# Attention and routed experts on one core: low halves of P at seven other blocks, a reordered preparation, magnitude sums as bfloat16 products

## The chip, the core and the metric

The kernel runs on one core of a Trainium2 chip. The metric is device time in microseconds (us), the median over runs of one launch. TensorE is called PE, VectorE DVE, ScalarE ACT, GpSimd POOL and SyncE SP, as in the profile.

## What is computed

Attention over 8 batches of 8 heads, 1152 keys and 576 pooled queries of 64 columns, and then a layer of 8 experts over the 4608 rows that come out of it, each row sent to one expert.

```python
q_pool = q.reshape(B, H, S // 2, 2, D).mean(axis=3)
scores = (1 / sqrt(D)) * q_pool @ k^T
attn = exp(scores - max); attn /= attn.sum() + 1e-9
x = (attn @ v) as 4608 rows of 512
e = argmax(x @ w_gate); weight = softmax(x @ w_gate)[e]
out = weight * sigmoid(x @ w_output_gate)[e] * (relu(x @ w1[e]) @ w2[e])
```

## The kernel before, in words

The attention works on 32 *pairs* (a batch and two of its heads), counted from 0 here. A pair has 18 *blocks* (two heads, nine chunks of 128 keys), and the main loop (lines 706 to 736) makes one *step* for each block. PE, DVE, ACT and POOL execute exactly in the order in which this loop writes their instructions (line 686), so the place of a call in a step is its place in the queue of its engine.

In a step, `scores` (lines 429 to 455) makes the scores of a block transposed (keys by queries) in one of two PSUM buffers, `sps0` for even blocks and `sps1` for odd ones: two products of high halves (L440) and two of low halves and maxima (L442). ACT takes the exponential P (L444). Its bfloat16 high half is read in place; the low half `pl` is P minus the high half. At most blocks POOL makes it from SBUF (L452), and then the PSUM buffer is free again once ACT has read it. At the blocks of the table `PLP` ACT takes the exponential a second time into PSUM (L446), and DVE subtracts (L449), at the start of the next step; the PSUM buffer is then free only after DVE. The block two later waits for it.

Beside this a step has: one or two maximum tiles (`mgen`, lines 355 to 388: scores of the pair after, 128 queries by 384 keys, two or three matmuls on L377 and a maximum by DVE on L378), which go through three small PSUM banks in rotation; zero to three groups of 15 products with V (`av`, L467 to L469), six steps behind the scores; and `rows` (line 407), which transposes a finished set of maxima (L412) through one of the three banks and hands it on to a split on DVE in the next step. In odd steps there are two maximum tiles, in even ones one. `norm` (L476 to L478) divides a finished head; `logits` and `router` (lines 512 to 647) are run by it, the router once in four pairs, in the pair after a batch's last, which makes the order repeat every four pairs.

`prep` (lines 143 to 347) prepares a pair ahead of its use, and a table gives the third of a step at which each of its parts is written out: `PREPF`, `PREP0` and `PREP` for pair 0, pair 1 and the rest. Its parts that matter here: `lk` loads q and k; `kabs` (L209) sums the magnitudes of k on ACT; `gk` (L213) adds that sum over partitions by an fp32 product with `blk`, in a bank that is held until `ksc(1)` (L220); `ks`, `kh`, `qs`, `qh` scale and round on ACT, `kl`, `qsum`, `ql` on POOL; `dk`, `dq`, `dl` send the results to their places through SP. For V, `amax` (ACT), `gmax` (an fp32 product with `onesf`, L319), `scale`, `vh` (ACT), `vs` and `vl` (POOL) do the same. The parts for k of pair n run during pair n-2, those for V during pair n-1.

After the attention the expert layer runs tile by tile; its code is not touched.

Of the kernel before, what the change touches and what calls it, by code (L numbers as in the profile page):

```python
# [23 lines left out]
PREP0 = ((0, 'lk'), (6, 'qsum'), (8, 'kabs'), (11, 'gk'), (12, 'ksc', 0), (12, 'ksc', 1), (13, 'ksc', 2), (14, 'ks', 0), (15, 'kh', 0), (15, 'qs'), (16, 'ks', 1), (17, 'kh', 1), (18, 'qh'), (18, 'kl'), (19, 'ql'), (19, 'dq', 0), (20, 'dq', 1), (22, 'qd'), (23, 'sk', 0, 0), (26, 'sk', 0, 1), (29, 'sk', 1, 0), (32, 'sk', 1, 1), (28, 'dl', 0), (29, 'dl', 1),  # L24
# [48 lines left out]
def attention(tc, qT, kT, vL, wg, keep, xrows, idscr, cum, pairs, setup, scat, init, exps):  # L73
    nc = tc.nc
    nb = len(pairs) // 4
    with ExitStack() as ctx:
# [66 lines left out]
        def prep(n, table):  # L143
# [531 lines left out]
        def prep_at(s, ph):  # L675
            u = 3 * (s + SLEAD) + ph
            for n in range(max(u // 54 - 2, 0), min(u // 54 + 2, NP)):
                r = u - 54 * n + min(3 * (LEAD - 15), 2 * n)
                if r == 0:
                    preps[n] = prep(n, PREP if n > 1 else PREP0 if n else PREPF)  # L680
                if n in preps:
                    for f in preps[n].pop(r, ()):
                        f()

        E = mybir.EngineType
        with tc.manual_schedule(engines={E.PE, E.DVE, E.Activation, E.Pool}):
# [55 lines left out]
def keep_tiles(tc, kp, NT, NP_):  # L742
    nc = tc.nc
# [512 lines left out]
```

## Time and profile before

| what | value |
|---|---|
| median of 3 runs | 1489.22 us (1487.53 to 1489.45) |
| profiled execution | 1491.79 us |
| its span, first to last instruction | 1489.9 us |
| mean granted PE clock | 0.991 of 2.4 GHz |
| busy share of PE, DVE, ACT, POOL | 96%, 75%, 68%, 63% |

The span of the profiled execution is 1.9 us shorter than its time. The attention's X at 968 us; the experts fill the rest. The pairs of the steady part follow each other every 28.6 to 30.2 us, with the pattern of four named above (pairs 12 to 15, for example, begin at 386.24, 415.61, 445.77 and 474.80 us). Matmuls overlap each other in the pipeline of PE, so what one costs the stream is read from the start of one to the start of the next, not from its duration.

### The profile page before, as it was taken

How to read it: one execution, taken by the hardware profiler on the slowest of the kernel's cores; microseconds unless marked ns; L12 is line 12 of the kernel's file. 1: busy time of each engine (PE TensorE's matmuls, PEld its weight loads, DVE VectorE, ACT ScalarE, POOL GpSimd, SP SyncE). 2: the span in 40 equal slices, each digit the busy share in tenths (PEclk: the TensorE clock that was granted, in tenths of full speed). 3: DMA queues.
4: the chain of work that ended last, by engine and by line, in shares of the span. 5: the costliest groups of instructions: out<-in, count | busy, mean ns of one | idle time of the engine just before them, and what ended most of it. 6: DMA issues, size and time to landing. Idle time of an engine off the chain costs nothing. (4 is left out here: it accounts for less than half of the span.)

```text
span 1489.9 us, 40217 instructions
## 1 busy us (share of the span) xinstructions
PE 1431.0 (96%) x16044; PEld 1144.2 (77%) x16044; DVE 1117.9 (75%) x2438; ACT 1012.9 (68%) x1723; POOL 939.1 (63%) x892
## 2 busy tenths in 40 slices
PE   7899999999999999999999999889999999999996
PEld 4677777777777777777777777777888888888874
DVE  8678787887887787788787787576778778777752
ACT  5777778777877877777877776644655556556542
POOL 3877888788889779878879888663333233333200
PEclk9999999999999999999999999999999999999998
DMA  5445344444443453444244433148636665453550
GB/s 190 123 122 145 102 134 123 115 118 118 117 137 102 115 143 98 117 134 121 86 137 125 126 92 96 58 148 330 231 105 232 228 233 213 171 186 122 218 186 8
DMA packets 92047, 212.57 MB, mean 143 GB/s; under 512 B 13356, under 2 KB 28924, under 8 KB 91854
## 3 DMA queue, kind: packets, MB, share of 16 engines
q1 hardware_dynamic: 81262, 188.35, 40.8%
q0 software_dynamic: 9152, 20.85, 4.1%
q8 instruction: 128, 2.10, 0.6%
q10 hardware_dynamic: 1440, 0.74, 0.2%
q14 instruction: 65, 0.53, 0.1%
HBM read 164.23 MB, written 23.02 MB: 126 GB/s over the span
## 5 line engine op out<-in xcount | busy, mean ns | idle before, releaser
L378 DVE TENSOR_REDUCE pm<-mp 128x1 f32<-128x384 f32 x864 | 449.5, 549 | 114.2 <-PE mp L377 109.6
L444 ACT ACTIVATE p<-sps 128x576 f32<-128x576 f32 x576 | 375.8, 653 | 199.6 <-PE sps L442 180.7
L452 POOL TENSOR_TENSOR pl<-p 128x576 f16<-128x576 f32 x383 | 437.8, 1146 | 112.5 <-ACT p L444 94.0
L377 PE MATMUL mp<-ka,qa 128*128 128x384 f16 x960 | 297.3, 326 | 12.0 <-DVE pm L378 6.5
L467 PE MATMUL av<-vt,p 128*128 128x65 f16 x2880 | 291.8, 193 | 0.2 <-DVE xb L478 0.2
L468 PE MATMUL av<-vt,p 128*128 128x64 f16 x2880 | 291.5, 194 | 0.0
L469 PE MATMUL av<-vt,pl 128*128 128x65 f16 x2880 | 291.1, 192 | 0.0
L467 PEld LDWEIGHTS <-p 128*128 128x128 bf16 x2880 | 265.8, 97 | 20.8 <-DVE xb L478 4.4
L468 PEld LDWEIGHTS <-p 128*128 128x128 bf16 x2880 | 264.4, 97 | 14.0
L469 PEld LDWEIGHTS <-pl 128*128 128x128 f16 x2880 | 264.3, 98 | 0.0
L377 PE MATMUL mp<-kb,qb 66*128 66x384 f16 x768 | 250.7, 326 | 0.8 <-DVE kb L251 0.5
L440 PE MATMUL sps<-qa,ka 128*128 128x288 f16 x1152 | 235.9, 286 | 11.2 <-DVE pl L449 9.8
L958 PE MATMUL hps<-x,w1h 128*128 128x512 f32 (+1 forms) x704 | 230.7, 389 | 7.6 <-DVE x L942 3.4
L442 PE MATMUL sps<-qb,kb 69*128 69x288 f16 x1152 | 235.7, 285 | 0.0
L449 DVE TENSOR_TENSOR pl<-sps,p 128x576 f16<-128x576 f32 x193 | 146.2, 757 | 38.1 <-ACT sps L446 29.8
L958 PE MATMUL hps<-x,w1l 128*128 128x256 f32 (+1 forms) x704 | 165.4, 276 | 0.0
L960 ACT COPY hs<-hps 128x512 f32<-128x512 f32 (+1 forms) x88 | 49.0, 557 | 171.0 <-PE hps L958 171.0
L958 PEld LDWEIGHTS hps<-x,w1l 128*128 128x128 f32 x704 | 132.3, 190 | 13.0
L958 PEld LDWEIGHTS hps<-x,w1h 128*128 128x128 f32 x704 | 122.8, 190 | 23.9 <-DVE x L942 4.0
L442 PEld LDWEIGHTS <-kb 69*128 69x128 f16 x1152 | 112.7, 98 | 29.2
L377 PEld LDWEIGHTS <-qa 128*128 128x128 f16 x960 | 95.2, 99 | 46.8 <-issue 9.5
L790 POOL DMA_INDIRECT ids<-idscr,riD x36 | 44.8, 1244 | 134.4 <-DMA out_dram<-y,ids 123.1
(243 smaller groups left out, 2810.5 us busy)
## 6 DMA issues: line engine op xcount, KB each, us to landing
raw2b<-in_w_dram SPq DMA_DIRECT2D x24, 1024.0 KB
raw1b<-in_w_dram SPq DMA_DIRECT2D x24, 1024.0 KB
raw1a<-in_w_dram SPq DMA_DIRECT2D x22, 1024.0 KB
raw2a<-in_w_dram SPq DMA_DIRECT2D x22, 1024.0 KB
vp<-in_vL_dram SPq DMA_DIRECT2D x32, 576.0 KB
qp<-in_qT_dram SPq DMA_DIRECT2D x31, 576.0 KB
kpf<-in_kT_dram SPq DMA_DIRECT2D x31, 576.0 KB
ka<-xk SPq DMA_DIRECT2D x120, 144.0 KB
```

The source lines that it names most:

```text
L377: nc.tensor.matmul(mp, lhsT=l, rhs=r, start=j == 0, stop=j == len(ops) - 1)
L378: nc.vector.tensor_reduce(out=pm[:, i:i + 1], in_=mp, axis=AX.X, op=ALU.max)
L440: nc.tensor.matmul(sps[:, j, 0:288], lhsT=ka[:, h, ks], rhs=qa[:, o + 288 * j:o + 288 * j + 288], start=True, stop=False)
L442: nc.tensor.matmul(sps[:, j, 0:288], lhsT=kb[:, h, ks], rhs=qb[:, h, 288 * j:288 * j + 288], start=False, stop=True)
L444: e_ = nc.scalar.activation(out=p32.rearrange("p (j n) -> p j n", j=2), in_=x, func=AF.Exp, scale=1.0 / 16)
L449: nc.vector.tensor_tensor(out=pl.rearrange("p (j n) -> p j n", j=2), in0=x, in1=ph.rearrange("p (j n) -> p j n", j=2), op=ALU.subtract)
L452: nc.gpsimd.tensor_tensor(out=pl, in0=p32, in1=ph, op=ALU.subtract)
L467: nc.tensor.matmul(av_[:, qb, 0:65], lhsT=hi, rhs=vt[:, h, c, 0:65], start=c == 0 and qb == 0, stop=False)
L468: nc.tensor.matmul(av_[:, qb, 0:64], lhsT=hi, rhs=vt[:, h, c, 66:130], start=False, stop=False)
L469: nc.tensor.matmul(av_[:, qb, 0:65], lhsT=lo, rhs=vt[:, h, c, 0:65], start=False, stop=c == NC - 1 and qb == 4)
L958: nc.tensor.matmul(hp[:, f, 0:n], lhsT=W1[l][g][:, c, fs], rhs=d['x'][:, c, 0:n], start=c == 0 and l == 0, stop=c == 3 and l == 0)
L960: nc.scalar.copy(out=hs, in_=hp[:, :, w:2 * w])
```

## The change

Five parts:

- `PLP`, the blocks whose low half DVE makes, becomes (1, 3, 5, 7, 9, 12, 13) in place of (1, 3, 7, 9, 11, 13): block 5 comes in, and block 12 takes the place of block 11. It holds for pairs 0 to 30; pair 31 has a table of its own, unchanged.
- From pair 4 on, `prep` runs by a new table: `kabs` at 8 in place of 14 (six thirds, two steps, earlier), `ksc(1)` directly behind `ksc(0)`, `qh` two thirds later, and the parts `scale`, `vh`, `vs`, `vl` of V shifted by one or two thirds. Pairs 2 and 3 keep the old table under the name `PREPE`.
- `dl` is cut in two, `dkl` (low half of k) and `dql` (low half of q), and k's goes first.
- `gk` and `gmax` multiply the upper 16 bits of the sums, read as bfloat16, by a `blk` and a `ones` of bfloat16.
- From step 54 (pair 3) on, `rows` is called right after the routers and ahead of the scores of its step, where it stood behind the maximum tiles.

```diff
-PREPK = (... (12, 'qsum'), (14, 'kabs'), (20, 'gk'), (21, 'ksc', 0), (22, 'ksc', 1), ... (31, 'qh'), ... (38, 'dl', 0), (40, 'dl', 1))
-PREPV = ((63, 'lv'), (82, 'amax', 0), (88, 'amax', 1), (93, 'gmax'), (94, 'scale', 0), (95, 'scale', 1), (99, 'scale', 2), (100, 'vh', 0), (101, 'vs', 0), (103, 'vl', 0), (107, 'vh', 1), (107, 'vs', 1), (110, 'vl', 1))
-PREP = PREPK + tuple((r + FWD, *x) for r, *x in PREPV)
+PREP = (... (8, 'kabs'), (12, 'qsum'), (20, 'gk'), (21, 'ksc', 0), (21, 'ksc', 1), ... (33, 'qh'), ... (38, 'dkl', 0), (38, 'dql', 0), (40, 'dkl', 1), (40, 'dql', 1)) + tuple((r + FWD, *x) for r, *x in ((63, 'lv'), (82, 'amax', 0), (88, 'amax', 1), (93, 'gmax'), (95, 'scale', 0), (96, 'scale', 1), (100, 'scale', 2), (101, 'vh', 0), (102, 'vs', 0), (104, 'vl', 0), (105, 'vh', 1), (108, 'vs', 1), (111, 'vl', 1)))
-PLP = (1, 3, 7, 9, 11, 13)
+PLP = (1, 3, 5, 7, 9, 12, 13)
-                nc.tensor.matmul(g[:, 0:1], lhsT=blk, rhs=ak[:, 0:1], start=True, stop=True)
+                nc.tensor.matmul(g[:, 0:1], lhsT=blk, rhs=ak.bitcast(BF16)[:, 1:2], start=True, stop=True)
-            def dl(h):
-                r = slice(64 * h, 64 * h + 64)
+            def dkl(h):
+                dmaf(kb[0:64, h], kp[64 * h:64 * h + 64])
+
+            def dql(h):
                 o = h * (NQ + 64)
-                dmaf(qa[64:128, o:o + NQ], yq[r])
-                dmaf(kb[0:64, h], kp[r])
+                dmaf(qa[64:128, o:o + NQ], yq[64 * h:64 * h + 64])
-                nc.tensor.matmul(g, lhsT=onesf, rhs=am, start=True, stop=True)
+                nc.tensor.matmul(g, lhsT=ones, rhs=am.bitcast(BF16).rearrange('p (h t) -> p h t', t=2)[:, :, 1], start=True, stop=True)
-                    preps[n] = prep(n, PREP if n > 1 else PREP0 if n else PREPF)
+                    preps[n] = prep(n, PREP if n > 3 else PREPE if n > 1 else PREP0 if n else PREPF)
+                if s >= 54 and (s % 2 == 0):
+                    rows()
                 pop()
                 if live:
                     next(sg)
...
-                if s < 54 or s % 2 == 0:
+                if s < 54:
                     rows()
-    blk = t('blk', [128, 128], F32)
+    blk = t('blk', [128, 128], BF16)
```

How the rows move, at the three places that matter. First ACT in blocks 0 to 3 of pair 15; `p` is written by the first exponential of a block, `vt` by `vh`, `kjunk` by `kabs`. Before:

```order
L444 ACTIVATE p_10542<-sps_10544 128x576
L332 ACTIVATE vt_147<-vp,sc 128x9x64
L444 ACTIVATE p_10588<-sps_10590 128x576
L446 ACTIVATE sps_10590<-sps_10590 128x2x288
L444 ACTIVATE p_10607<-sps_10609 128x576
L209 ACTIVATE kjunk,ak<-kpf 128x1152
L444 ACTIVATE p_10658<-sps_10660 128x576
```

And in the change:

```order
L444 ACTIVATE p_10557<-sps_10559 128x576
L332 ACTIVATE vt_147<-vp,sc 128x9x64
L208 ACTIVATE kjunk,ak<-kpf 128x1152
L444 ACTIVATE p_10604<-sps_10606 128x576
L446 ACTIVATE sps_10606<-sps_10606 128x2x288
L444 ACTIVATE p_10626<-sps_10628 128x576
L444 ACTIVATE p_10673<-sps_10675 128x576
```

`kabs` has moved from behind the exponential of block 2 to ahead of both exponentials of block 1.

Second PE around the scores of block 12 of pair 15; `mp` is a maximum tile, L540 are the logits' products, L412 is the transpose of `rows`, `sps` the scores of block 12. Before:

```order
L442 LDWEIGHTS kb_122
L442 MATMUL sps_10998<-qb_131,kb_122 128x288
L377 LDWEIGHTS qa_129
L377 MATMUL mp_11005<-ka_126,qa_129 128x384
L377 LDWEIGHTS qb_132
L377 MATMUL mp_11005<-kb_123,qb_132 128x384
L412 MATMUL tp<-ident,m_10911 5x128
L467 LDWEIGHTS p_10765
```

And in the change:

```order
L377 LDWEIGHTS qb_132
L377 MATMUL mp_11003<-kb_123,qb_132 128x384
L540 MATMUL tp<-xh,wgt 128x256
L540 MATMUL tp<-xl,wgt 128x256
L412 MATMUL tp<-ident,m_10927 5x128
L440 LDWEIGHTS ka_125
L440 MATMUL sps_11016<-qa_128,ka_125 128x288
```

The transpose has moved from behind the maximum tile of the step to ahead of its scores. The three banks rotate: before, L412 took the bank of the second maximum tile of the step ahead; now it takes that of the first, and the maximum tile of its own step takes the second's.

Third DVE in blocks 5 and 6 of pair 13; L218 (L217 in the change) and L220 (L219) are `ksc(0)` and `ksc(1)`, L615 to L617 are the router's. Before:

```order
L478 TENSOR_TENSOR xb<-av_9113,r 128x5x64
L218 TENSOR_SCALAR tp<-tp 128x1
L378 TENSOR_REDUCE pm<-mp_9402 128x1
L220 TENSOR_SCALAR ik<-tp 128x1
L378 TENSOR_REDUCE pm<-mp_9407 128x1
L223 RECIPROCAL ik<-ik 128x1
L615 TENSOR_REDUCE tp<-exg_155 128x5
L616 SCALAR_TENSOR_TENSOR tp<-sl,tp 128x5
```

And in the change:

```order
L478 TENSOR_TENSOR xb<-av_9125,r 128x5x64
L217 TENSOR_SCALAR tp<-tp 128x1
L219 TENSOR_SCALAR ik<-tp 128x1
L378 TENSOR_REDUCE pm<-mp_9416 128x1
L378 TENSOR_REDUCE pm<-mp_9420 128x1
L222 RECIPROCAL ik<-ik 128x1
L449 TENSOR_TENSOR pl<-sps_9407,p_9405 128x576
L615 TENSOR_REDUCE tp<-exg_155 128x5
```

`ksc(1)`, which frees the bank of `gk`, now stands ahead of both maxima, and the low half of block 5 is new behind them.

## Rows read from the trace of the kernel before

**Rows 1.** The page's busy times: engine, busy us, share of the span, instructions.

```profile
PE 1431.0 (96%) x16044; PEld 1144.2 (77%) x16044; DVE 1117.9 (75%) x2438; ACT 1012.9 (68%) x1723; POOL 939.1 (63%) x892
```

**Rows 2.** Windows of pairs 12 to 15, summed: busy us of each engine.

```profile
sum 117.20, PE 115.12 PEld 90.02 DVE 93.30 ACT 91.40 POOL 96.66; mean PE 28.78 PEld 22.51 DVE 23.32 ACT 22.85 POOL 24.16
```

**Rows 3.** Who PE waited for, 120 to 940 us: total us, times, longest us.

```profile
PE mp L377 <- DVE pm L378: 6.3, 13, 0.6
PE mp L377 <- DVE xl L530: 3.7, 14, 0.3
PE tp L523 <- DVE pm L378: 2.7, 9, 0.3
```

**Rows 4.** Timeline of ACT, pair 15, blocks 0 to 3: start us, duration us, instruction.

```profile
476.09 0.77 ACT L332 ACTIVATE vt<-vp,sc 128x576 f16<-128x576 f32 x1
477.22 0.65 ACT L444 ACTIVATE p<-sps 128x576 f32<-128x576 f32 x1 [0.36 <-PE sps L442]
477.77 0.65 ACT L446 ACTIVATE sps<-sps 128x576 f32<-128x576 f32 x1
...
478.99 1.15 ACT L209 ACTIVATE kjunk<-kpf 128x1152 f16<-128x1152 f32 x1
480.04 0.19 ACT L209 ACTIVATION_READ_ACCUMULATOR kjunk<-kpf 128x1 f32 x1
480.22 0.65 ACT L444 ACTIVATE p<-sps 128x576 f32<-128x576 f32 x1
```

**Rows 5.** Timeline of ACT, pair 15, blocks 6 and 7.

```profile
485.00 0.65 ACT L444 ACTIVATE p<-sps 128x576 f32<-128x576 f32 x1 [0.57 <-PE sps L442]
485.54 1.43 ACT L227 ACTIVATE kpf<-kpf,ik 128x576 f32<-128x576 f32 x2
486.88 0.64 ACT L444 ACTIVATE p<-sps 128x576 f32<-128x576 f32 x1
```

**Rows 6.** Timeline of DVE, pair 15: the low half of block 1.

```profile
478.52 0.76 DVE L449 TENSOR_TENSOR pl<-sps,p 128x576 f16<-128x576 f32 x1
```

**Rows 7.** Timeline of PE, pair 15: the scores of block 3.

```profile
479.53 0.41 PE L440 MATMUL sps<-qa,ka 128*128 128x288 f16 x2
```

**Rows 8.** Timeline of PE, pair 13: the second maximum tile of block 5's step.

```profile
425.81 0.32 PE L377 MATMUL mp<-ka,qa 128*128 128x384 f16 x1 [0.65 <-DVE pm L378]
```

**Rows 9.** Timeline of DVE, pair 13: the maximum that this tile waited for.

```profile
425.20 0.56 DVE L378 TENSOR_REDUCE pm<-mp 128x1 f32<-128x384 f32 x1
```

**Rows 10.** Timeline of DVE, pair 14: the start of norm, after its wait.

```profile
454.65 0.22 DVE L476 TENSOR_SCALAR r<-av,sc 128x5 f32<-128x5 f32 x1 [0.95 <-PE tp L213]
```

**Rows 11.** Timeline of PE, pair 15: the logits' products, the scores of block 12.

```profile
494.55 0.28 PE L540 MATMUL tp<-xl,wgt 128*128 128x256 f32 x1
494.67 0.42 PE L440 MATMUL sps<-qa,ka 128*128 128x288 f16 x2
```

**Rows 12.** Timeline of DVE, pair 15: the two maxima of block 11's step.

```profile
494.29 1.02 DVE L378 TENSOR_REDUCE pm<-mp 128x1 f32<-128x384 f32 x2
```

**Rows 13.** Timeline of PE, pair 15: the fp32 product gk and what follows.

```profile
482.87 0.36 PE L213 MATMUL tp<-ak,blk 128*128 128x1 f32 x2
483.09 0.41 PE L440 MATMUL sps<-qa,ka 128*128 128x288 f16 x2
```

**Rows 14.** Timeline of PE, pair 13: the router's small bfloat16 products.

```profile
421.65 0.24 PE L601 MATMUL tp<-ohb,ones 128*128 128x32 bf16 x4
421.75 0.18 PE L602 MATMUL tp<-cum,ones 128*128 128x40 bf16 x1
```

**Rows 15.** Timeline of PE, pair 15: a maximum tile of block 9's step, after its wait.

```profile
490.65 0.48 PE L377 MATMUL mp<-ka,qa 128*128 128x384 f16 x2 [0.27 <-DVE xl L530]
```

**Rows 16.** Timeline of PE, pair 15: the fp32 product gmax and what follows.

```profile
498.47 0.28 PE L319 MATMUL tp<-am,onesf 128*128 128x2 f32 x2
498.62 0.32 PE L377 MATMUL mp<-ka,qa 128*128 128x384 f16 x1
```

**Rows 17.** Timeline of DVE, pair 15: the two maxima of block 13's step.

```profile
497.54 1.02 DVE L378 TENSOR_REDUCE pm<-mp 128x1 f32<-128x384 f32 x2 [0.23 <-PE mp L377]
```

More of the change, by code (lines that the diff above doesn't have):

```diff
@@ L23 @@
 RI = 7
-PREP0 = ((0, 'lk'), (6, 'qsum'), (8, 'kabs'), (11, 'gk'), (12, 'ksc', 0), (12, 'ksc', 1), (13, 'ksc', 2), (14, 'ks', 0), (15, 'kh', 0), (15, 'qs'), (16, 'ks', 1), (17, 'kh', 1), (18, 'qh'), (18, 'kl'), (19, 'ql'), (19, 'dq', 0), (20, 'dq', 1), (22, 'qd'), (23, 'sk', 0, 0), (26, 'sk', 0, 1), (29, 'sk', 1, 0), (32, 'sk', 1, 1), (28, 'dl', 0), (29, 'dl', 1),
+PREP0 = ((0, 'lk'), (6, 'qsum'), (8, 'kabs'), (11, 'gk'), (12, 'ksc', 0), (12, 'ksc', 1), (13, 'ksc', 2), (14, 'ks', 0), (15, 'kh', 0), (15, 'qs'), (16, 'ks', 1), (17, 'kh', 1), (18, 'qh'), (18, 'kl'), (19, 'ql'), (19, 'dq', 0), (20, 'dq', 1), (22, 'qd'), (23, 'sk', 0, 0), (26, 'sk', 0, 1), (29, 'sk', 1, 0), (32, 'sk', 1, 1), (28, 'dkl', 0), (28, 'dql', 0), (29, 'dkl', 1), (29, 'dql', 1),
         (53, 'lv'), (71, 'amax', 0), (74, 'amax', 1), (81, 'gmax'), (82, 'scale', 0), (85, 'scale', 1), (90, 'scale', 2), (93, 'vh', 0), (93, 'vs', 0), (96, 'vh', 1), (97, 'vl', 0), (100, 'vs', 1), (104, 'vl', 1))
@@ L28 @@
          (78, 'amax', 0), (82, 'amax', 1), (99, 'gmax'), (100, 'scale', 0), (100, 'scale', 1), (100, 'scale', 2), (103, 'vh', 0), (103, 'vs', 0), (106, 'vh', 1), (107, 'vl', 0), (109, 'vs', 1), (113, 'vl', 1))
-PREPK = ((0, 'lk'), (12, 'qsum'), (14, 'kabs'), (20, 'gk'), (21, 'ksc', 0), (22, 'ksc', 1), (23, 'ksc', 2), (25, 'ks', 0), (26, 'ks', 1), (27, 'kh', 0), (29, 'kh', 1), (29, 'kl'), (29, 'qs'), (30, 'dk', 0), (31, 'dk', 1), (31, 'qh'), (33, 'dq', 0), (34, 'dq', 1), (34, 'ql'), (37, 'qd'), (38, 'dl', 0), (40, 'dl', 1))
-PREPV = ((63, 'lv'), (82, 'amax', 0), (88, 'amax', 1), (93, 'gmax'), (94, 'scale', 0), (95, 'scale', 1), (99, 'scale', 2), (100, 'vh', 0), (101, 'vs', 0), (103, 'vl', 0), (107, 'vh', 1), (107, 'vs', 1), (110, 'vl', 1))
 FWD = 9
-PREP = PREPK + tuple((r + FWD, *x) for r, *x in PREPV)
+PREP = ((0, 'lk'), (8, 'kabs'), (12, 'qsum'), (20, 'gk'), (21, 'ksc', 0), (21, 'ksc', 1), (23, 'ksc', 2), (25, 'ks', 0), (26, 'ks', 1), (27, 'kh', 0), (29, 'kh', 1), (29, 'kl'), (29, 'qs'), (30, 'dk', 0), (31, 'dk', 1), (33, 'qh'), (33, 'dq', 0), (34, 'dq', 1), (34, 'ql'), (37, 'qd'), (38, 'dkl', 0), (38, 'dql', 0), (40, 'dkl', 1), (40, 'dql', 1)) + tuple((r + FWD, *x) for r, *x in ((63, 'lv'), (82, 'amax', 0), (88, 'amax', 1), (93, 'gmax'), (95, 'scale', 0), (96, 'scale', 1), (100, 'scale', 2), (101, 'vh', 0), (102, 'vs', 0), (104, 'vl', 0), (105, 'vh', 1), (108, 'vs', 1), (111, 'vl', 1)))
+PREPE = ((0, 'lk'), (12, 'qsum'), (14, 'kabs'), (20, 'gk'), (21, 'ksc', 0), (22, 'ksc', 1), (23, 'ksc', 2), (25, 'ks', 0), (26, 'ks', 1), (27, 'kh', 0), (29, 'kh', 1), (29, 'kl'), (29, 'qs'), (30, 'dk', 0), (31, 'dk', 1), (31, 'qh'), (33, 'dq', 0), (34, 'dq', 1), (34, 'ql'), (37, 'qd'), (38, 'dkl', 0), (38, 'dql', 0), (40, 'dkl', 1), (40, 'dql', 1)) + ((72, 'lv'), (91, 'amax', 0), (97, 'amax', 1), (102, 'gmax'), (103, 'scale', 0), (104, 'scale', 1), (108, 'scale', 2), (109, 'vh', 0), (110, 'vs', 0), (112, 'vl', 0), (116, 'vh', 1), (116, 'vs', 1), (119, 'vl', 1))
 PREP0 = tuple((r + FWD, *x) for r, *x in PREP0)
@@ L341, in prep @@
             P = functools.partial
-            fns = dict(lf=lf, fsel=fsel, qsv=qsv, klh=klh, sk=sk, sl=sl, sq0=sq0, sq1=sq1, qd=qd, kabs=kabs, gk=gk, ksc=ksc, ks=ks, khs=khs, qs=qs_, lk=lk, lv=lv, kh=kh, kl=kl, qsum=qsum, qh=qh, ql=ql, dk=dk, dq=dq, dl=dl, amax=amax, gmax=gmax, scale=scale, vh=vh, vs=vs, vl=vl)
+            fns = dict(lf=lf, fsel=fsel, qsv=qsv, klh=klh, sk=sk, sl=sl, sq0=sq0, sq1=sq1, qd=qd, kabs=kabs, gk=gk, ksc=ksc, ks=ks, khs=khs, qs=qs_, lk=lk, lv=lv, kh=kh, kl=kl, qsum=qsum, qh=qh, ql=ql, dk=dk, dq=dq, dkl=dkl, dql=dql, amax=amax, gmax=gmax, scale=scale, vh=vh, vs=vs, vl=vl)
             out = {}
@@ L715, in attention @@
                 for r in routers:
-                    if not s % 2 or not live or not r[1]:
+                    if (not s % 2) or not live or not r[1]:
                         r[1] = next(r[0], 0)
+                if s >= 54 and (s % 2 == 0):
+                    rows()
                 pop()
```

## The prediction

> **What bounds it now.** I read the busy times first, then four pairs as a window, then PE's waits, then timelines of single steps. PE is busy 96% of the span [rows 1], and over four pairs 115.12 of 117.20 us; DVE, ACT and POOL have about a fifth of that stretch free [rows 2]. So in the steady part PE's stream of matmuls is the bound, and the three others matter where they make PE wait at one place. Those places are few: from 120 to 940 us PE waited 6.3 us for maxima that had to leave a bank, 3.7 us for the logits' subtraction and 2.7 us ahead of a transpose whose bank a maximum still held [rows 3]. PE waited for no low half made by POOL. From this follow the three questions for each part: does it shorten PE's stream, does it shorten one of these waits, does it make a new one.
>
> **kabs at block 0.** In pair 15 the half `vh(1)` starts at 476.09, and the first exponential of block 1 at 477.22, as soon as its scores are there; the second follows at 477.77 and `kabs` comes only at 478.99, in a hole before block 3's exponential [rows 4]. The low half of block 1 starts .75 us behind the second exponential, at 478.52, and ends at 479.28 [rows 6]; the scores of block 3, which need that PSUM buffer, start at 479.53 [rows 7]. A wait on DVE's end takes PE some .06 us more (a maximum that ended at 425.76 let PE start at 425.81, [rows 8, 9]), so there is a reserve of 479.53 - 479.34 = .2 us. In the change `kabs` stands ahead of both exponentials of block 1. After `vh(1)` an ACT instruction of that size lets the next start .67 us later ((486.88 - 485.54)/2, [rows 5]): `kabs` at 476.76, its accumulator read 1.05 us later (480.04 - 478.99), the exponential .09 to .18 us after that (480.22 - 480.04 is the upper end, since that exponential had also waited for its scores; the lower end is that consecutive instructions overlap by .1 us, as 477.77 - 477.22 = .55 for one of .65 us) [rows 4]. That is 477.90 to 477.99 in place of 477.22, .68 to .77 us late. Less the reserve, **PE stands still .48 to .57 us ahead of block 3**, in each of pairs 2 to 29 (the new table serves preparations 4 to 31). I take .5, and .38 in the seven pairs of the router (5, 9, ... 29), where block 3 starts .12 us later already: 21 x .5 + 7 x .38 = 13.2 us. The work behind it on DVE (maxima, split) is late too, but is wanted only .4 us or more after.
>
> The old place cost nothing: the exponential of block 3 came when its scores did. So nothing is got back there. Some of the 13.2 us may be absorbed in pairs 6, 10, ... 26: there `norm` starts only after DVE has been idle .95 us [rows 10], in pair 14 long after the last product with V was issued, so a PE that comes up to .5 us later could find the same start. 0 to 3.5 us; I take 2.
>
> **rows ahead of the scores.** In pair 15 the logits' last product starts at 494.55 and block 12's scores at 494.67 [rows 11]. Now the transpose stands there, and its bank is that of the first maximum tile of block 11's step. The two maxima take 494.29 to 495.31, so the first ends near 494.29 + .55 = 494.84 [rows 12]; with .06 us for the signal PE waits until 494.90, **.22 us**, and the banks rotate alike in all four kinds of pairs. It is the same kind of wait as that of L523 [rows 3]. The transpose's own time only moves. 28 pairs (3 to 30): 6.2 us; the bounds are 0 (the maximum comes sooner) and .3 a pair, 8.4. In block 2 the tile whose bank it takes is three products older, and it waits for nothing.
>
> **The two products.** The fp32 `gk` holds PE from 482.87 to 483.09, .22 us [rows 13]. The router's bfloat16 products of similar size follow each other every .025 us (421.65 to 421.75 for four, [rows 14]). So `gk` saves .195 us. The Trainium skill (FP8 and Floating Point Precision, TensorE Precision Notes) has a true fp32 product as four passes; a bfloat16 one would then be a quarter, .055, and the saving .165, an estimate. The trace shows two matmuls for each product, and the router's rows give the smaller price. What a saving is worth depends on the next wait: in three of four kinds of pairs PE waits in block 9 for the logits' subtraction [rows 15], at the end of a chain on ACT that begins with the scaling behind `ksc(2)` and block 6's exponential, so only what also moves that chain counts. I take .15 us in 14 pairs and .1 in the seven where `norm` starts late, 2.8 us. In the seven pairs of the router PE waits .65 us for a bank ahead of the second tile of block 5 [rows 8]; there `ksc(1)` now frees `gk`'s bank at once, .4 us sooner, of which the new low half of block 5 takes back .1: .3 x 7 = 2.1 us. `gmax` costs 498.62 - 498.47 = .15 us [rows 16], but the next tile needs the bank of a maximum that ends at 497.54 + 1.02 = 498.56 [rows 17]: PE would wait there instead. 0, at most .12 x 30 = 3.6 us.
>
> **Seven low halves.** One more on DVE (.76 us) and one more exponential on ACT (.65 us) a pair lie beside PE, four of each in 117.20 us of which DVE and ACT have 24 and 26 free [rows 2]; the second exponential of block 5 falls into a hole on ACT, idle for .57 us between the exponentials of blocks 5 and 6 [rows 5]. Block 7 may wait up to .3 us for it, ahead of the wait in block 9 that is there anyway. If that cover goes, 28 x .1, some 3 us. POOL's relief (1.15 us a pair) is worth 0, since PE did not wait for POOL. The later `qh`, `dkl` ahead of `dql` and the shifted parts of V: 0; their users come blocks later.
>
> **The first pairs.** In pairs 0 to 2 the two products count in full, 3 x (.195 + .12) = .9 us, and block 11's buffer is free sooner in pair 0, where ACT is late: by about one subtraction and one exponential, 1.4 us, less what block 5's new ones take there. -2 us, an estimate between -3 and +1.
>
> **Sum.** 13.2 - 2 + 6.2 - 2.8 - 2.1 - 0 - 2 = +10.5 us. The profiled execution took 1491.79 us, of which 1489.9 are the span; that is 2.6 us above the median of the runs, 1489.22. By the sum a profile would come to about 1502 and the median to 1499.7. I say **1499**, a little under, as more of the new waits may be absorbed than the one that I counted.
>
> **Rivals.**
> 1. *PE's saving decides, the new waits do not come* (faster). The Trainium skill (Perfetto Trace Analysis, Identifying the Most-Contended Engine) has one improve the most contended engine first; that is PE, and by that rule the change is a gain. As a mechanism here: `kabs` ends in time for block 1 or block 3 has more reserve than .2 us, and the transpose's bank is free. It decides at .2 us of ACT's .68. Then -2.8 - 2.1 - 2 and up to 3.6 of `gmax`: -7 to -10.5, about 1480. For it: PE's 96%. Against it: the order on ACT is fixed, and its durations don't vary.
> 2. *One of the two new waits alone* (no change). If only the transpose's comes, 6.2 - 7 = -1; if only block 3's, and half is absorbed behind other waits, 6.6 - 7 = 0. About 1489.
> 3. *k's load is not there at the earlier kabs* (much slower). Then ACT would stand still at block 0, and all exponentials behind it. From .5 us more a pair on, 28 x .5: 1513 or more. Against it: no wait of `kabs` for its load shows in the steady part, and the load is written out two and two thirds steps ahead.
>
> **Chances.** Forecast .72, rival 1 .14, rival 2 .11, rival 3 .03. A difference of .2% (3 us) is about what a measurement can tell from none. Faster: .15; within .2%: .12; slower: .73. The forecast's own range: all bounds at the low end give 13.2 - 3.5 + 0 - 7 - 3.6 - 1 = -2, at the high end 15 + 8.4 + 3 - 4 + 1 = +23, but these ends don't meet; 1493 to 1506. The whole range leaves out rival 1 and what is above: 1486 to 1506.
>
> **What would show it.** In the profile after: a wait of L440 for the low half L449, some .5 us in each pair, at block 3; a wait of L412 for a maximum of .2 us in each; the scores behind `gk` .2 us nearer; block 5's wait in router pairs at .25 or less. If PE does not wait at block 3, the largest term is wrong, and the time falls under 1490.

## The result, and the profile after

The changed kernel takes **1509.23 us** (median of 4 runs, 1507.45 to 1510.18) against 1488.38 us of the kernel before in the same session: a ratio of 1.0143 [1.0122, 1.0164], slower by some 21 us. Slower was forecast, but by about half as much: 1499, with a range that ended at 1506.

| what | before | after |
|---|---|---|
| median | 1488.38 us | 1509.23 us |
| profiled execution, its span | 1491.79, 1489.9 us | 1509.89, 1508.1 us |
| first scores to last product with V | 938.6 us | 954.4 us |
| last product with V to the end | 518.2 us | 521.0 us |
| pairs 12, 13, 14 (start to start) | 29.37, 30.16, 29.03 us | 30.36, 30.30, 29.42 us |
| pair 11, of the same kind as 15 | 28.64 us | 29.43 us |
| granted clock, mean | 0.991 | 0.991 |

The last product with V ends at 971.7 us in the kernel before, so X is complete after that and not at 968 us. In the windows of pairs 12 to 15 the granted clock is 1.00 of 2.4 GHz in both kernels.

The page's busy times of the changed kernel (beside [rows 1]):

```profile
PE 1436.8 (95%) x15980; PEld 1137.9 (75%) x15980; DVE 1139.0 (76%) x2469; ACT 1023.4 (68%) x1754; POOL 904.7 (60%) x861
```

PE is busy for a smaller share of the span than before, and the others stay far from theirs: DVE and ACT have 1 to 2% more to do, POOL 4% less. The time must lie in waits. Who PE waited for in the steady part, 120 to 955 us (beside [rows 3]; total us, times, longest us):

```profile
PE sps L440 <- DVE pl L449: 6.2, 19, 0.6
PE tp L565 <- DVE inv L326: 3.5, 7, 0.5
PE mp L377 <- DVE ik L219: 3.4, 7, 0.5
PE tp L523 <- DVE pm L378: 2.7, 9, 0.3
PE tp L412 <- DVE pm L378: 2.3, 7, 0.3
PE mp L377 <- DVE pm L378: 0.4, 1, 0.4
```

The first row is the wait on the low half that was forecast, in 19 pairs. The second was not forecast: the router's transposes wait for `inv`, which is `scale(1)` of V. The third is the wait for `gk`'s bank in block 5 of the router's pairs, .49 us where [rows 8] have .65. The fifth was forecast at another block. Two things about this list: it counts only time in which PE was wholly idle, and since a matmul's end is modelled some .16 us behind the start of the next, a PE that starts .47 us late shows .31; and short stretches are left out. So the waits for `xl` [rows 3] are not gone: block 9 still waits .30 us from start to start, where it waited .43. I read sizes from start to start.

**Block 3.** ACT in blocks 0 to 3 of pair 14 (beside [rows 4]; the pair starts at 450.91, pair 15 of [rows 4] at 474.80):

```profile
452.21 0.77 ACT L332 ACTIVATE vt<-vp,sc 128x576 f16<-128x576 f32 x1
452.87 1.15 ACT L208 ACTIVATE kjunk<-kpf 128x1152 f16<-128x1152 f32 x1
453.92 0.19 ACT L208 ACTIVATION_READ_ACCUMULATOR kjunk<-kpf 128x1 f32 x1
454.02 0.64 ACT L444 ACTIVATE p<-sps 128x576 f32<-128x576 f32 x1
454.55 0.65 ACT L446 ACTIVATE sps<-sps 128x576 f32<-128x576 f32 x1
```

Then DVE's low half of block 1 (beside [rows 6]):

```profile
455.30 0.76 DVE L449 TENSOR_TENSOR pl<-sps,p 128x576 f16<-128x576 f32 x1 [0.62 <-ACT sps L446]
```

and PE's scores of block 3 (beside [rows 7]):

```profile
456.11 0.42 PE L440 MATMUL sps<-qa,ka 128*128 128x288 f16 x2 [0.31 <-DVE pl L449]
```

The exponential of block 1 stands 3.11 us behind the pair's start in place of 2.42, .69 us late, and the scores of block 3 5.20 us in place of 4.73: .47 us, as worked out in the forecast (.48 to .57). It is there in 19 pairs from 4 on. In the seven pairs of the router PE waits as long one block earlier, for the bank of the rows' transpose:

```profile
423.98 0.27 PE L412 MATMUL tp<-ident,m 128*4 128x128 f32 x1 [0.32 <-DVE pm L378]
```

**Block 12.** PE in pair 14 (beside [rows 11]), and the two maxima of block 11's step on DVE (beside [rows 12]):

```profile
471.03 0.27 PE L540 MATMUL tp<-xl,wgt 128*128 128x256 f32 x1
471.39 0.28 PE L412 MATMUL tp<-ident,m 128*5 128x128 f32 x1
471.50 0.41 PE L440 MATMUL sps<-qa,ka 128*128 128x288 f16 x2
```

```profile
470.78 1.02 DVE L378 TENSOR_REDUCE pm<-mp 128x1 f32<-128x384 f32 x2 [0.39 <-PE mp L377]
```

The transpose starts when the first of the two maxima is done (470.78 + .55 = 471.33, and .06 for the signal), .36 us behind the product ahead of it, where the scores of [rows 11] came .12 behind: .24 us of waiting, forecast .22.

**gk.** PE at block 4 of pair 14 (beside [rows 13]): .03 us from `gk` to the scores, where the fp32 product took .22. The forecast had .025.

```profile
459.46 0.17 PE L212 MATMUL tp<-ak,blk 128*128 128x1 bf16 x1
459.49 0.40 PE L440 MATMUL sps<-qa,ka 128*128 128x288 f16 x2
```

**Block 6 of the pairs 4k+2 (6, 10, ... 26), on which the forecast leaned.** The first instruction of `norm` in pair 14 (beside [rows 10], where DVE had waited .95 us):

```profile
459.67 0.22 DVE L476 TENSOR_SCALAR r<-av,sc 128x5 f32<-128x5 f32 x1 [0.34 <-PE tp L212]
```

It starts .04 us behind the end of the last product with V ahead of it, as it does (.07 at most) in the other kinds of pairs in both kernels. In the kernel before, it started .65 to .72 us behind that end in the six pairs 4k+2, and PE waited .50 us at block 6 in consequence. That late start is gone, and it is not the changed stream of PE that takes it up. In the run with the seven low halves alone (below) PE's stream up to that place is the one of the kernel before, and `norm` still comes .62 us sooner:

```profile
455.18 0.22 DVE L476 TENSOR_SCALAR r<-av,sc 128x5 f32<-128x5 f32 x1 [0.34 <-PE av L469]
```

**Block 16, where nothing was forecast.** DVE in blocks 15 and 16 of pair 14, after:

```profile
476.79 0.15 DVE L324 TENSOR_SCALAR tp<-tp 128x2 uint32<-128x2 uint32 x1
476.86 0.20 DVE L476 TENSOR_SCALAR r<-av,sc 128x5 f32<-128x5 f32 x1
477.10 0.19 DVE L477 RECIPROCAL r<-r 128x5 f32<-128x5 f32 x1
477.32 0.49 DVE L478 TENSOR_TENSOR xb<-av,r 128x320 f32<-128x320 f32 x1
477.73 0.15 DVE L326 TENSOR_SCALAR inv<-tp 128x2 f32<-128x2 f32 x1
```

The same place before, rows that were not shown:

```profile
471.39 0.15 DVE L324 TENSOR_SCALAR tp<-tp 128x2 uint32<-128x2 uint32 x1
471.57 0.16 DVE L326 TENSOR_SCALAR inv<-tp 128x2 f32<-128x2 f32 x1
471.65 0.21 DVE L476 TENSOR_SCALAR r<-av,sc 128x5 f32<-128x5 f32 x1
```

`scale(0)` and `scale(1)` were one third of a step later in the new table, and so `scale(1)` (L326) fell behind the three instructions of `norm`. It frees `gmax`'s bank: .18 us behind L324 before, .94 us behind it now. PE needs that bank for block 16's maximum tile, whose step is

```profile
477.52 0.41 PE L442 MATMUL sps<-qb,kb 69*128 69x288 f16 x2
477.93 0.32 PE L377 MATMUL mp<-ka,qa 128*128 128x384 f16 x1
```

.41 us from L442 to L377, where .25 is usual: .16 to .17 us of waiting in three pairs of four. In the fourth the router's transposes take that bank:

```profile
417.28 0.49 PE L565 MATMUL tp<-ident,lT 32*128 32x32 f32 x5 [0.50 <-DVE inv L326]
```

There block 16 gets some back, and .37 us remain.

**The account of the two traces**, from start to start, before to after: block 3, or the transpose at block 2: 19 x .47 + 7 x .48 = +12.3 us; block 12: 28 x .23 = +6.4; the bank of `gmax`: 19 x .17 + 7 x .37 + .4 in pair 3 = +6.2; `gk`, `ksc(1)`, the low half of block 5 and the earlier `norm`, which make blocks 4 to 10 shorter by .12, .36, .47 and .12 us in the four kinds of pairs: -6.9, of which 6 x .50 = 3.0 us are `norm`'s; less time at blocks 14 and 15 of the router's pairs (see the last section): -1.8; the rest (first and last pairs, pairs 15, 20 and 26) about -1.2. That is +15, and up to the last product with V the traces differ by 15.4. Behind it lie another 2.8.

### The profile page after: what moved, and what is told of

The parts are those of the page before. It is cut to its first block, busy times and chain, and to the rows that moved or that the text cites. A ratio compares the mean times of both kernels' runs of the same rounds, so it can differ in the third digit from the quotient of the medians.

```text
span 1508.1 us, 40060 instructions
## 1 busy us (share of the span) xinstructions
PE 1436.8 (95%) x15980; PEld 1137.9 (75%) x15980; DVE 1139.0 (76%) x2469; ACT 1023.4 (68%) x1754; POOL 904.7 (60%) x861
## 5 line engine op out<-in xcount | busy, mean ns | idle before, releaser
L452 POOL TENSOR_TENSOR pl<-p 128x576 f16<-128x576 f32 x352 | 403.6, 1148 | 155.3 <-ACT p L444 146.6
L377 PE MATMUL mp<-ka,qa 128*128 128x384 f16 x960 | 297.3, 326 | 7.3 <-DVE ik L219 3.4
L377 PE MATMUL mp<-kb,qb 66*128 66x384 f16 x768 | 250.7, 326 | 0.8 <-DVE kb L250 0.5
L442 PE MATMUL sps<-qb,kb 69*128 69x288 f16 x1152 | 235.8, 285 | 0.0
L449 DVE TENSOR_TENSOR pl<-sps,p 128x576 f16<-128x576 f32 x224 | 168.1, 750 | 38.5 <-ACT sps L446 36.8
L446 ACT ACTIVATE sps<-sps 128x576 f32<-128x576 f32 x224 | 145.5, 649 | 0.0
L442 PEld LDWEIGHTS <-kb 69*128 69x128 f16 x1152 | 112.7, 98 | 29.1
L377 PEld LDWEIGHTS <-qa 128*128 128x128 f16 x960 | 92.6, 96 | 46.9 <-issue 8.8
```

The lines of the kernel that those rows point to most:

```text
L377: nc.tensor.matmul(mp, lhsT=l, rhs=r, start=j == 0, stop=j == len(ops) - 1)
L442: nc.tensor.matmul(sps[:, j, 0:288], lhsT=kb[:, h, ks], rhs=qb[:, h, 288 * j:288 * j + 288], start=False, stop=True)
L446: e_ = nc.scalar.activation(out=x, in_=x, func=AF.Exp, scale=1.0 / 16)
L449: nc.vector.tensor_tensor(out=pl.rearrange("p (j n) -> p j n", j=2), in0=x, in1=ph.rearrange("p (j n) -> p j n", j=2), op=ALU.subtract)
L452: nc.gpsimd.tensor_tensor(out=pl, in0=p32, in1=ph, op=ALU.subtract)
```

## The experiments

All times are medians; ratios with their 95% interval are to the kernel before in the same session, 1489.0 us with the first two sets of four (in 15 to 17 runs, 1484.7 to 1492.7) and 1493.4 with the last four kernels, which ran on two further chips.

**kabs back.**

```diff
-PREP = ((0, 'lk'), (8, 'kabs'), (12, 'qsum'), (20, 'gk'),
+PREP = ((0, 'lk'), (12, 'qsum'), (14, 'kabs'), (20, 'gk'),
```

> The changed kernel with one number put back: the sum of magnitudes of K (kabs) stands at 14 again, behind the block's exponentials instead of ahead of them. My theory: the wait of block 3's scores on the low half of block 1 (0.48 us in three of four pairs, and 0.48 us of the rows' transpose at block 2 in the fourth) comes from kabs alone, 28 times 0.48 us = 13.4 us; it goes, and the time is 1494 to 1498 us against 1509.2 us of the changed kernel. Rival (part of it is taken up elsewhere, as the prediction had it with 2 us or more): 1500 us or above. Rival that the matmul records overstate it: over 1505 us.

1499.77 us, 1.0066 [1.0051, 1.0081]: 9.5 us less than the changed kernel, not the 11 to 15 of my theory, and on the rival's edge. Its trace shows why. Block 3 waits in no pair, as expected. But in the router's pairs the wait at block 2 stays (waits of PE, 120 to 920 us; there is no row for `pl` L449 any more):

```profile
PE tp L412 <- DVE pm L378: 2.2, 7, 0.3
```

So that wait is not of `kabs`; it belongs to the transpose's new place and had only stood ahead of `kabs`' own. What `kabs` costs is 19 x .47 + 7 x .13 = 9.8 us, and 9.5 were measured.

**The transpose back.**

```diff
-                if s >= 54 and (s % 2 == 0):
-                    rows()
...
-                if s < 54:
+                if s < 54 or s % 2 == 0:
                     rows()
```

> The changed kernel with the rows' transpose (L412) put back behind the maximum tiles of its step. My theory: the wait of 0.23 us at block 12 in 28 pairs (6.5 us) goes, and so does the 0.48 us at block 2 of the router's pairs, but there block 3's own wait on the low half of block 1 comes back in its place; so 1501 to 1504 us. Rival (the transposes in the old place wait for their own maxima as long as they do now): 1507 us or above.

1506.65 us, 1.0124 [1.0104, 1.0143]: 2.6 us less, just short of the rival. The interval overlaps that of the changed kernel, so the 2.6 us by themselves are not clear of noise; the two traces differ by 1.6 us in pairs 4 to 29 and by 1.3 us in pair 30. In the router's pairs block 3's own wait is back, .35 us, in the place of the transpose's, as expected. The wait at block 12 is gone, but another has come at block 13. DVE there (of this kernel, pair 14):

```profile
474.48 0.76 DVE L449 TENSOR_TENSOR pl<-sps,p 128x576 f16<-128x576 f32 x1 [0.34 <-ACT sps L446]
475.16 0.27 DVE L416 TENSOR_SCALAR mr<-tp 5x128 f16<-5x128 f32 x1
475.46 0.27 DVE L417 SCALAR_TENSOR_TENSOR mr<-mr,tp 5x128 f16<-5x128 f16 x1
```

and PE:

```profile
475.39 0.33 PE L377 MATMUL mp<-kb,qb 66*128 66x384 f16 x1
475.79 0.42 PE L540 MATMUL tp<-xh,wgt 128*128 128x320 f32 x1
```

The logits' product takes the bank of the rows' transpose, which L417 frees, at 475.73. L417 stands behind the low half of block 12, one of the seven, and so L540 starts .40 us behind L377 where .165 is usual: .23 us. The earlier transpose and the low half of block 12 cost the same .23 us; each hides the other.

**V's numbers back, all thirteen, and two of them.**

```diff
-(95, 'scale', 0), (96, 'scale', 1), (100, 'scale', 2), (101, 'vh', 0), (102, 'vs', 0), (104, 'vl', 0), (105, 'vh', 1), (108, 'vs', 1), (111, 'vl', 1)
+(94, 'scale', 0), (95, 'scale', 1), (99, 'scale', 2), (100, 'vh', 0), (101, 'vs', 0), (103, 'vl', 0), (107, 'vh', 1), (107, 'vs', 1), (110, 'vl', 1)
```

> The changed kernel with the thirteen numbers of V's part of the preparation put back. My theory: the later inverse of V's scale (L326 now behind the norm) holds the PSUM bank of gmax longer, and that is the 0.17 us wait of the maximum tile of block 16 in three pairs and the 0.37 us of the router's transpose in the fourth, 0.86 us in four pairs, 6 us in all: 1502 to 1504 us. The prediction's view (the shifted parts of V cost nothing, and the excess over its sum lies elsewhere): 1508 us or above.

```diff
-(95, 'scale', 0), (96, 'scale', 1),
+(94, 'scale', 0), (95, 'scale', 1),
```

> The changed kernel with two numbers of V's part put back, the steps scale(0) and scale(1) at 94 and 95; the reciprocal, vh, vs and vl stay at the new numbers. My theory: V's cost of 7 us is all in the bank of gmax, which scale(1) frees, so all of it goes: 1501 to 1504 us, as with all thirteen numbers put back (1502.2). Rival (the later vh, vs or vl carry some of it): 1505 us or above.

1502.19 us, 1.0093 [1.0076, 1.0110], and 1502.07 us, 1.0084 [1.0066, 1.0102]: 7.0 and 7.2 us less. The two early steps carry all of it, and the shifts of the reciprocal, `vh`, `vs` and `vl` are free. In both the row for L565 is gone from PE's waits, and block 15 of the pairs 4k is 1.67 us long, as before, for 2.24 in the changed kernel.

**All three back.** The three edits above (the thirteen numbers) in one kernel.

> The changed kernel with all three put back: kabs at 14, the rows' transpose behind the maximum tiles, V's part of the table as before. What is left of the change is the seven low halves, the bfloat16 products of sums, ksc(1) at 21, qh at 33 and the order of the copies of low parts. My theory: the three costs add (13.4 + 6.5 + 6 us), so 1509 - 26 = 1483 us, between 1480 and 1485, below the kernel before. Rival (the costs overlap, since a wait removed lets the next one come up): 1486 to 1492 us. Rival (the rest of the change costs something too, such as the late start of the experts): above 1492 us.

1488.46 us, 0.9996 [0.9984, 1.0007]: 20.8 us less than the changed kernel and the time of the kernel before. The three make up all of the loss (singly 9.5 + 2.6 + 7.0 = 19.1). My theory, that the rest gains 6 us, fell; the rest does nothing on balance. The next two runs ask why, for two of its parts; `qh` and the order of the copies were not run by themselves.

**The bfloat16 products alone,** in the kernel before:

```diff
-nc.tensor.matmul(g[:, 0:1], lhsT=blk, rhs=ak[:, 0:1], start=True, stop=True)
+nc.tensor.matmul(g[:, 0:1], lhsT=blk, rhs=ak.bitcast(BF16)[:, 1:2], start=True, stop=True)
-nc.tensor.matmul(g, lhsT=onesf, rhs=am, start=True, stop=True)
+nc.tensor.matmul(g, lhsT=ones, rhs=am.bitcast(BF16).rearrange('p (h t) -> p h t', t=2)[:, :, 1], start=True, stop=True)
-    blk = t('blk', [128, 128], F32)
+    blk = t('blk', [128, 128], BF16)
```

> The kernel before with the two products of sums of magnitudes in bfloat16 and nothing else of the change. My theory: block 4 loses the 0.20 us that its product gk loses in the changed kernel's trace, in 28 pairs, 5.6 us, and nothing takes it up: 1482 to 1485 us against 1489. Rival (undoing kabs, rows and V in the changed kernel gave only the time of before, because the products' gain is taken up by the next wait): 1487 to 1490 us.

1484.35 us, 0.9964 [0.9950, 0.9977]: 4.6 us faster than the kernel before, in the range of the theory. Here the saving is not taken up: block 4 is .19 us shorter in every kind of pair. (In its trace the early `norm` takes another .42 us off block 6 of the pairs 4k+2, which the theory did not have.)

**The seven low halves alone,** in the kernel before:

```diff
-PLP = (1, 3, 7, 9, 11, 13)
+PLP = (1, 3, 5, 7, 9, 12, 13)
```

> The kernel before with the seven low halves (blocks 1, 3, 5, 7, 9, 12, 13 for 1, 3, 7, 9, 11, 13) and nothing else. My theory, from the changed kernel with three parts put back: block 7 waits 0.23 us for the low half of block 5, block 9 waits 0.13 us less, and the product of the logits waits 0.23 us more at block 13 behind the low half of block 12; 0.33 us in 28 pairs is 9 us, and some 0.6 us in each router pair and the pair behind it come back (4 us): 1492 to 1496 us. The prediction's view (nothing): 1488 to 1490 us. Rival (fewer low halves on POOL bring a gain): under 1487 us.

1496.88 us, 1.0055 [1.0035, 1.0075]: 7.9 us slower, a little above my range, and well off the prediction's nothing. The place at block 13 is right (.34 us longer from block 13 to 14 in every pair). Block 7 does not wait here: with the fp32 `gk` PE comes there .2 us later. So in the changed kernel, outside the router's pairs, the low half of block 5 is what eats `gk`'s saving: block 4 is .20 shorter, block 7 waits .23, and block 9's wait is .13 less. Of the 7.9 us the traces show only 2.9 in pairs 4 to 29, since the late `norm` is gone here and block 6 of the pairs 4k+2 is .50 us shorter, as is block 14 of the router's pairs by .20. The place is shown, the size is not. The products' 4.6 us and the seven low halves' 7.9 us, with the .17 us that the earlier `ksc(1)` saves in seven pairs, leave what the run with all three back shows to within 3 us.

**No low half of block 1, kabs still early.**

```diff
-PLP = (1, 3, 5, 7, 9, 12, 13)
+PLP = (3, 5, 7, 9, 12, 13)
```

> The changed kernel with the low half of block 1 back on POOL (six low halves by VectorE), kabs still at 8. My theory: kabs costs only through the chain second exponential of block 1, its low half, score buffer, scores of block 3. Without that low half the chain is gone and block 3 doesn't wait: 1497 to 1501 us, as with kabs at 14 (1499.8). Rival (kabs makes the first exponential late as well, or POOL, 1.15 us for a low half, becomes late for the sums of products): 1505 us or above.

1497.80 us, 1.0056 [1.0039, 1.0073]: 11.4 us less than the changed kernel, with `kabs` where the change puts it. The scores of block 3 wait in no pair. Some 1.3 us of it lie in pairs 0 to 2, where `kabs` is not early. The chain is as drawn: `kabs` is dear only because a second exponential and a subtraction stand behind it and a score buffer behind these.

**kabs early, alone,** in the kernel before:

```diff
-PREPK = ((0, 'lk'), (12, 'qsum'), (14, 'kabs'), (20, 'gk'),
+PREPK = ((0, 'lk'), (8, 'kabs'), (12, 'qsum'), (20, 'gk'),
```

> The kernel before with kabs at 8 from pair 2 on and nothing else: the dearest part of the change alone. My theory: 0.48 us at block 3 in the pairs 4k and 4k+3 and 0.13 us in the router pairs 4k+1, where another wait stands ahead; in the pairs 4k+2 it shortens the wait of 0.5 us that block 6 of the kernel before has there (as the prediction's 2 us have it). Some 1.1 us in four pairs, 7.7 us: 1495 to 1498 us. Rival (nothing is taken up in the pairs 4k+2): 1499 to 1501 us. Rival (the prediction's full 13.2 us): above 1501 us.

1509.39 us against 1493.44, 1.0099 [1.0082, 1.0115]: 16 us slower, which by the number alone is the last case, the full 13.2 us. The trace bears it out only in part. In the pairs 4k+2 `norm`'s wait is shorter, as in the theory (pair 14, beside [rows 10]),

```profile
462.77 0.23 DVE L476 TENSOR_SCALAR r<-av,sc 128x5 f32<-128x5 f32 x1 [0.60 <-PE tp L213]
```

and block 6 waits .16 us where it waited .50: .34 of block 3's .48 come back in pair 14. In most of the others less does, as the second matmul of `gk` starts up to .35 us later at block 4; the six pairs are .14 to .49 us longer, 2.0 us in all for 2.9 at block 3. In the router's pairs nothing hides the wait here, .48 to .49, as the transpose is at its old place. Pairs 4 to 29 together are 12.0 us longer. Another 2 us are in pair 0, which I had not thought of, and where ACT never pauses (ACT, pair 0):

```profile
40.12 0.77 ACT L332 ACTIVATE vt<-vp,sc 128x576 f16<-128x576 f32 x1
40.78 1.16 ACT L209 ACTIVATE kjunk<-kpf 128x1152 f16<-128x1152 f32 x1
41.84 0.20 ACT L209 ACTIVATION_READ_ACCUMULATOR kjunk<-kpf 128x1 f32 x1
41.93 0.65 ACT L444 ACTIVATE p<-sps 128x576 f32<-128x576 f32 x1
```

The period of pair 0 is 32.52 us for 30.47. `kabs` has at most a part of this: in this execution the granted clock is at its lower level, 1.2 GHz, from 42 to 49 us (.56, .50, .50 and .73 of 2.4 GHz in the four stretches of 2 us from 42 to 50), and at 1.00 in the profile of the kernel before; blocks 5 and 6 take 5.4 us there for 3.0. PE had waited 1.74 us at block 3 shortly ahead of the fall, but it does so in the kernel before too. The change avoids `kabs`' part by its table for pairs 2 and 3. The remaining 4 us lie outside the pairs. The first scores come 1.8 us later; there too the clock differs, .50 from 10 to 20 us for .66. The part behind the last product is 1.8 us longer, and that I can't tie to the edit. Four of the five runs have a mean clock of .987 or .988; the fifth has .993 and took 1504.5 us, where the four runs of the kernel before at .992 took 1491.4 to 1494.2. So some 12 us and a part of pair 0 are shown for this edit, more than the theory's 7.7 and less than the 16.

**The transpose back, and block 11 for block 12.** The edit of the transpose's run, and

```diff
-PLP = (1, 3, 5, 7, 9, 12, 13)
+PLP = (1, 3, 5, 7, 9, 11, 13)
```

> The changed kernel with the rows' transpose back behind the maximum tiles, and block 11 in place of block 12 among the seven low halves. My theory: the wait of the transpose at block 12 (0.23 us) and the wait of the logits' products at block 13 (0.23 us, for the split L417 of the transposed maxima, which stands behind the low half of block 12 on VectorE) stand in for each other, so that putting the transpose back alone brought only 2.6 us; with both put back neither wait is there: 1500 to 1503 us. Rival (the transpose's place is worth 2.6 us and no more): 1506 us or above.

1505.32 us against 1493.45, 1.0072 [1.0056, 1.0087]. Set against the kernel before that is +11.9 us, where the kernel with the transpose alone put back stood at +17.6: 5.7 us for block 11, as in theory. Its trace shows less. The pairs 4k, 4k+2 and 4k+3 are .19 us shorter than with block 12, as they should be, but in the router's pairs .15 us more is spent at blocks 14 and 15, so that only some 3 us can be pointed at. The sign is settled, the size not.

**A move that the change does not make.** The waits that are left in the run with the products alone led to ACT at block 9: the copy of the logits' rows (L527), on which `xl` and with it block 9's maximum tile wait [rows 15], stands behind the scaling of q (L230):

```profile
395.92 1.23 ACT L276 CAST xk<-kpf 128x576 f16<-128x576 f32 x2
397.05 0.78 ACT L230 ACTIVATE qs<-qs,ik 128x576 f32<-128x576 f32 x1
397.73 0.36 ACT L527 CAST xh<-tp 128x256 fp32r<-128x256 f32 x1
```

With the products and `ksc(1)` at 21, `qs` goes behind that copy, or behind both copies of the logits:

```diff
-(21, 'ksc', 0), (22, 'ksc', 1), ... (29, 'kl'), (29, 'qs'), (30, 'dk', 0), (31, 'dk', 1), (31, 'qh'), (33, 'dq', 0)
+(21, 'ksc', 0), (21, 'ksc', 1), ... (29, 'kl'), (30, 'qs'), (30, 'dk', 0), (31, 'dk', 1), (33, 'qh'), (33, 'dq', 0)
```

> The kernel before with the bfloat16 products, ksc(1) at 21 (from the change), and one move that the change does not make: qs at 30 for 29 and qh at 33 for 31, so that ScalarE copies the transposed rows of the logits (L527) ahead of the scaling of q at block 9. My theory: the wait of block 9's maximum tile for xl (0.34 us in the pairs of the run with the products alone) goes, since that copy stands 0.8 us behind qs there; with ksc(1) 0.26 us less in each router pair; 1474 to 1478 us. Rival (the second copy, at block 10, is now behind qs and makes block 11 wait as long): 1481 to 1484 us.

> As the run with qs at 30, but with qs at 33 (behind both copies of the logits' rows), qh behind it and ql at 36. My theory: neither copy waits for the scaling of q, and the copies of q are still in time: 1472 to 1477 us. Rival (POOL's subtraction ql, 1.3 us, comes so late that its low halves are late, or the loads of q are late for the next pair's maxima): 1482 us or above.

1480.49 us, 0.9915 [0.9899, 0.9931], with `qs` at 30, and 1483.53 us, 0.9940 [0.9926, 0.9954], with `qs` at 33; both against 1493.4. The first is 13 us faster than the kernel before and by the two ratios some 34 us faster than the changed one, and **beats both**. ACT there:

```profile
395.96 1.23 ACT L276 CAST xk<-kpf 128x576 f16<-128x576 f32 x2
397.09 0.37 ACT L527 CAST xh<-tp 128x256 fp32r<-128x256 f32 x1
397.36 0.66 ACT L444 ACTIVATE p<-sps 128x576 f32<-128x576 f32 x1
397.90 0.78 ACT L230 ACTIVATE qs<-qs,ik 128x576 f32<-128x576 f32 x1
```

The copy comes .6 us sooner, and block 9's wait for `xl` is gone from PE's waits. A part is given back, as the rival had it: the second copy is now behind `qs`, and the logits' product at block 11 waits .21 us. And `norm` starts late again in the pairs 4k+2 (.65 us or more behind its product), where block 6 is .36 us longer than with the products alone. With `qs` at 33 block 11 is 1.69 us long for 1.54 with `qs` at 30. Both theories were made from 1489 us for the kernel before; counted from 1493.4, the first is met (-13 us for -11 to -15) and the second failed (-10 for -12 to -17).

## Why the prediction was wrong, point by point

- **kabs at block 0, 13.2 us.** The mechanism, the place and the size hold: .69 us late on ACT, .47 us at block 3. It is there in 26 pairs, not 28: from pair 4 on `kabs` starts 1.97 us behind the pair's start, but in pair 2 at 3.54, behind those exponentials, and in pair 3 at 1.30, with `vh(1)` behind these exponentials instead of ahead of them. And in the router's pairs only .13 of .48 is its own. `kabs` is worth 9.5 us by the run that takes it back.
- **"I take 2" for what is absorbed in pairs 6, 10, ... 26.** This step failed: the pairs 4k+2 of the changed kernel show .47 us at block 3 like the others, and nothing is absorbed. The .95 us that DVE stood idle ahead of `norm` [rows 10] were taken for a property of these pairs. They were a late start, .65 us behind the product that `norm` needs, and in the changed kernel, as in the runs with the products alone and with the low halves alone, it is .04 us. Where `norm` is still late, in the run with `kabs` alone, .9 us of 2.9 are absorbed. (The upper bound of 3.5 us was also one pair too many: six pairs give 3 us.)
- **rows ahead of the scores, 6.2 us.** The wait is .24 us against .22, in 28 pairs. Taken back alone it returns 2.6 us, since the low half of block 12 waits behind it.
- **The two products, -4.9 us, and the seven low halves, 0.** Together -6.9 us in blocks 4 to 10 of the trace. That this is better than forecast is luck: 3.0 us of it are the late `norm` that went, and 3.9 are left for 4.9. In the router's pairs block 5's wait shows as .49 us and not as .25 or less, since PE comes there .19 us sooner behind the shorter `gk`; blocks 4 and 5 together give .35 us for the .3 of the sum. The saving of `gk` was sized at .195 us, and .19 was measured. The Trainium skill (FP8 and Floating Point Precision, TensorE Precision Notes) has true fp32 as four passes; by that the bfloat16 `gk` would take .055 us, an estimate. The trace shows .03, nearer to the router's rows. `gmax` gives nothing at block 14, as forecast. Of the seven low halves, that of block 5 came as priced: block 7 waits .23 us, and .13 come back at block 9. That of block 12 was not seen: it holds up the logits' product at block 13, which makes the edit by itself slower (+7.9 us), and it costs nothing in the whole change only because the rows' earlier place hides it.
- **The first pairs, -2 us.** Pairs 0 to 2 are 1.0 us shorter in the trace, within the stated bounds.
- **"The shifted parts of V: 0; their users come blocks later."** This is the step that failed most: 7.0 us by the run that takes it back, 6.2 by the two traces. The users of V do come later, and moving `vh`, `vs` and `vl` is free. But `scale(1)` has another user, the PSUM bank that it frees, and a third of a step carried it across `norm`. I had asked that question of `gk` and `ksc(1)`, and not of `gmax` and `scale(1)`, which are the same construction. The Trainium skill (Perfetto Trace Analysis, Optimization Strategy) has the same gap, repeated, on the engine that should be saturated as a possible sign that PSUM for the next tile ran out. The trace agrees: .17 us in each of 19 pairs.
- **The step from the profile to the median.** I took the 2.6 us by which the profiled execution of before exceeded the median off the forecast of after. The profile of after exceeds its median by only .7 us. The profile of before was one of that kernel's longer executions (its runs took 1484.7 to 1492.7 us). It holds the late `norm` and the late blocks 14 and 15, 4.8 us that the profile of after does not have; whether the shorter executions of the kernel before have them too is not shown.

From span to span the changed kernel is 18.2 us longer, 7.7 more than the sum of 10.5. By the two traces this is +6.2 for V, +1.1 at block 3 (12.3 for 13.2 - 2), +.2 for the rows, -2.0 for the products and low halves, -1.8 at blocks 14 and 15, +.8 for the first pairs and the rest, and +2.8 behind the last product with V: +7.3. The other 2.6 us of the 10.2 between forecast and result are the step to the median. The 2.8 us and the 2.6 us were not tried by any run.

Of the rivals none came. The first, a PE that decides by its busy share, had its test in the run with the products alone: where nothing else is moved, PE's saving counts (4.6 us); beside four other edits it does not decide.

## What to carry to other kernels

When engines run in a written order, ask of every moved instruction not only who reads its result, but which buffer it frees and who takes that buffer next; a third of a step was enough to put three instructions ahead of a release. An idle stretch in one trace is not yet a reserve: ask what ends it, and whether that is still there once the other edits are in; here the one that was to absorb 2 us went with edits that do not touch it. And an edit taken back alone shows less than it costs when a second wait stands behind the first. Before an instruction is moved ahead of others, look which of these feed a chain that ends in the bound engine: here one instruction of 1.05 us cost nothing behind the exponentials and .47 us a pair ahead of them.

## What was not expected of the hardware

- Executions of one kernel differ in parts that no edit touches, and partly with the granted clock. In the fourteen profiles the first scores come at 32.6 to 33.2 us in eight and at 34.4 to 35.0 in six; from 10 to 20 us the clock is .66 to .69 of 2.4 GHz in the eight and .50, the lower level, in the six. In the kernel before (.66) and the one with `kabs` alone (.50) PE had no matmul from 8 to 12 us. The part from the last product with V to the end takes 516.3 to 521.0 us, in no relation to the edits, while most pairs of the steady part repeat within .02 us in a trace. A single profile's span is therefore good to some 3 us here, and the length of a pair to far less. Of 17 runs of the kernel before on one chip, the five with a mean clock of .987 took 1492.2 to 1492.5 us, the twelve with .989 to .994 took 1486.2 to 1490.6.
- `norm` starts .65 to .77 us behind its last product in the pairs 4k+2 of two kernels (before, and `qs` at 30), .30 to .62 in two others (`kabs` alone, `qs` at 33), and .04 in the other ten. At block 14 of the router's pairs PE starts .1 to .5 us later in four kernels, different from pair to pair, and not at all in most others (1.43 us from block 14 to 15 in the changed kernel, 1.59 to 1.82 in most of these pairs before). Both come and go with edits far from them. An indirect DMA of POOL (L638) runs beside `norm` in the kernel before, but in the run with the low halves alone it runs there too. The cause was not tried and stays open.
